# Attention steps in pairs at half as many places of the mixture, one pipeline over three batches, and a set order of the first loads

## The chip, the cores and the metric

The kernel runs on one core of one Trainium2 chip. The metric is device time in microseconds (us) of one execution, as a median of runs. Engines: PE (TensorE), DVE (VectorE), ACT (ScalarE), POOL (GpSimd) and SP (SyncE, which issues most DMAs).

## What is computed

Three layers in a row. The inputs of the mixture (w_a, w_b, w_out) are 64-bit floats, all others 32-bit.

```python
# attention: 4 batches, 8 heads, 576 positions, 64 per head
scores = q @ k.T / 8, masked           # heads 0-3: the last 32 positions
                                       # heads 4-7: every 32nd position before
x = softmax(scores) @ v                # -> 2304 tokens x 512
# gated mixture
x = (x @ w_a) * (x @ w_b) @ w_out      # 512 -> 1536 -> 512
# eight experts, top two of each token
noisy = x @ w_gate + log1p(exp(x @ w_noise)) * noise
for e, w in top2(noisy) with softmax weights w:
    out[token] += w * (relu(x @ w1[e]) @ w2[e])   # 512 -> 1024 -> 512
```

## The kernel before

**Attention.** A batch is four units, each two heads, in the order HPS = (0, 2, 1, 3): hp 0 and 1 have the local mask (96 positions by 128 keys, three at a time), hp 2 and 3 the strided one (72 by 72, four at a time). A unit's steps are T (four, transposes of q and k), Q (four, scores, and behind the second of each half E, the softmax), P (four, transposes of the weights) and PV (two). att_pipe is a generator that yields behind each step and interleaves a unit's with the next one's. Masks are added either by a PE matmul with identb (batch 0) or by a DVE addition (batches 1 to 3, the tensor_add in Q). Where "wide" holds, E is one subtraction, one exponential and one sum over a whole half in place of single rows of ACT with an accumulator.

**Mixture.** Tokens go in chunks: c = 0 to 3 are 512 tokens of one batch each, c = 4 the 4 x 64 left over. A chunk has twelve stages f: stage_a makes pa and pb (12 matmuls each: mm3 multiplies high and low parts in three matmuls), and a*pb in high and low parts gh, gl; stage_b adds to po (12 more, 6 in chunk 4) for the stage before. The 64-bit weights are loaded raw (load_raw, 512 KB or 1 MB) and split on DVE and ACT into high and low parts (split64), 48 steps of it during batch 0 and chunk 0 (conv_to).

**Places.** PE's order is written by hand: stage_a and stage_b call point(), six times a stage: in the middle of pa, behind pa, in the middle of pb, behind pb, and twice in stage_b. Each call advances the attention queue attq by one step, and every third call (every second in chunk 4) the queue bgq, in which finish (X: transposes of the mixture's rows, G: the gate's matmul, then the routing, R: ranks of the tokens in each expert, and eight scatters of the slots to a table in memory), load_expert and fetch (a load of the table, gathers of tokens, S: their transposes) take turns. So the attention of batch c + 1 runs inside chunk c; what is left of it is run at stage 11.

**Other orders.** Except in batch 0, where the scheduler sets it, PE runs what the program says; the other engines' order is set by the scheduler from its own estimate. Expert weights go through two slots st0 and st1 (load_unit, L146; ACT makes the high part, L149, DVE the low part, L150) into the ring slots w0 to w5, which the mixture's stages 0 to 7 hold before. load_expert(0) joins bgq at (c, f) = (4, 5), fetch(0) at (4, 8). Batch 0's q, k, v come through st slots and four more. PSUM tiles of attention, X, G, R and S share the two banks of tag "t"; batch 0's go to the four of tag "o", but for P and PV.

Of the kernel before, what the change touches and what calls it, by code (L numbers as in the profile page):

```python
# [32 lines left out]
def attention_moe_kernel(ctx: ExitStack, tc: tile.TileContext, q, k, v, w_a, w_b, w_out,  # L33
# [165 lines left out]
    class Unit:  # L199
# [36 lines left out]
        def T(self, i):  # L236
# [11 lines left out]
            if self.wide and i // 2:  # L248
# [8 lines left out]
        def Q(self, half, x):  # L257
            n, g, m = self.n, self.g, self.m
            msk = maskAB[:, half:half + 3, :] if self.local else maskS[:, None, :].to_broadcast([72, 4, 72])
            if x == 0:  # L260
                self.s[half] = self.tile("s", [n, 2, g, m])
                st = self.tile("sst", [96, 1 if self.wide else 2, 8])
                self.mx, self.sm[half] = st[:n, 0, 0:2 * g], st[:n, 0 if self.wide else 1, 0:2 * g]
# [3 lines left out]
            if self.pemask:  # L267
                nc.tensor.matmul(ps, identb[:n, :n], msk, start=True, stop=False)
            for ii in range(g):
# [4 lines left out]
                else:  # L274
# [3 lines left out]
                                 start=not self.pemask, stop=not self.pemask or ii == g - 1)  # L278
            mx = self.mx[:, g * x:g * x + g]
            if self.pemask:  # L280
# [10 lines left out]
        def E(self, half):  # L291
            n, g = self.n, self.g
# [3 lines left out]
            if not self.pemask:  # L296
                nc.vector.tensor_reduce(mx, s3, axis=AX.X, op=OP.max)
            if self.wide:
                if not self.pemask:
# [40 lines left out]
    def att_pipe(us, ahead, done=None):  # L340
# [8 lines left out]
        if ahead == 2:  # L349
            us[1].load_v()  # L350
        for n, u in enumerate(us):
# [39 lines left out]
        if done:  # L391
            done(u)
# [111 lines left out]
    pair = [None]  # L504

    def store_x2(c, ps, j):
        if j % 2 == 0:
            pair[0] = rpool.tile([128, 2, DM], F32, name="row", tag=f"row{j // 2}")
        row = pair[0][:, j % 2, :]
# [13 lines left out]
    bgq, attq = [], []  # L523
# [10 lines left out]
    def pump():  # L534
        advance(attq)
        advance(bgq)

    def drain():
        while bgq or attq:
# [22 lines left out]
    def load_m1():  # L562
# [17 lines left out]
    cp = m1.enter_context(tc.tile_pool(name="conv", bufs=1))  # L580
    a1 = ExitStack()
    p1 = a1.enter_context(tc.tile_pool(name="att1", bufs=1, reuse_waits="tile"))
    nraw = [0]

    def next_of(n):
        nraw[0] += 1
        return nraw[0] % n

    conv_room["raw"] = lambda m: cp.tile([128, 1024, 2], I32, name="raw", tag=f"u{next_of(2)}")[:, 0:m, :]
    cts = []  # L590

    def ct_tile(m):

        if not cts:
            ct = cp.tile([128, 2, 1024], I32, name="ct", tag="u2")
            cts.extend((ct[:, 0], ct[:, 1]))
        cts.append(cts.pop(0))
        return cts[-1][:, 0:m]

    conv_room["ct"] = ct_tile  # L600
    conv = load_m1()
    nconv = [0]
# [9 lines left out]
    def p1tile(name, shape):  # L612
        if name in ("ql", "kl", "vl"):
            nslot[0] += 1
            i = nslot[0] % 6
            return stage.tile(shape, F32, name=name, tag=f"st{i}") if i < 2 else \
                p1.tile(shape, F32, name=name, tag=f"qkv{i}")
        return p1.tile(shape, F32, name=name, tag=name, bufs=P1BUFS[name])

# [355 lines left out]
```

## Time and profile before

| | |
|---|---|
| median of the runs | 1170.57 us (1167.08, 1170.57, 1170.78) |
| profiled execution: time, span | 1169.36 us, 1167.6 us |
| PE busy | 1102.8 us, 94% of the span |
| DVE, ACT, POOL busy | 525.3, 418.0, 144.0 us |
| batch 0 up to the first stage of chunk 0 | 0 to 48.7 us |
| chunk 0 | 48.7 to 220.2 |
| chunks 1, 2 (with attention) | 220.2 to 357.5, 357.5 to 494.0 |
| chunk 3 (without) | 494.0 to 599.0 |
| chunk 4 | 599.0 to the first expert matmul, 676.6 |
| expert passes | 676.6 to the end |

Times are from the span's start. A stage's bounds are the first pa matmul of each. The chain of work that ended last is PE for 78% of the span, DMA for 10%, DVE for 7%. A row of the timeline has start, length, engine, line, operation, out<-in, shape and count; in brackets the idle time of the engine just before and what ended it.

### The profile page before, as it was taken

The page shows a single profiled execution, that of the slowest core. Times are in us where ns is not written, and L with a number is a line of the kernel's source. Part 1 is how long each engine was busy: PE and PEld are TensorE (multiplying, and loading weights), DVE is VectorE, ACT ScalarE, POOL GpSimd, SP SyncE. Part 2 cuts the span into 40 slices and gives each one's busy share as a digit, 9 for nine tenths or more (in the row PEclk, how much of TensorE's full clock was granted, in tenths as well). Part 3 has the DMA queues.
Part 4 walks back from the last instruction along what each step waited for, and adds up shares of the span by engine and source line. Part 5 has one row for each costly group of instructions (what it writes and reads, how often), then busy time and mean ns, then how long its engine had stood idle before and what let it go on. Part 6 is the DMA issues. An engine that isn't in the chain of part 4 may idle for free.

```text
span 1167.6 us, 16084 instructions
## 1 busy us (share of the span) xinstructions
PE 1102.8 (94%) x6381; PEld 927.2 (79%) x6381; DVE 525.3 (45%) x1109; ACT 418.0 (36%) x936; POOL 144.0 (12%) x136
## 2 busy tenths in 40 slices
PE   6768999999999999999999699999999998999996
PEld 5546777777777777888888589988999897988995
DVE  5688985355435465211326361245342434242111
ACT  5666664233223242221225251244242424232111
POOL 0000000000200002000020313231030313021112
PEclk9969999999999999999999999999999999999998
DMA  8544522101111111730013643266253626242023
GB/s 183 176 123 153 177 80 65 61 22 32 37 26 58 31 36 49 268 112 1 1 37 110 127 126 57 46 194 183 78 139 92 156 82 166 66 116 40 11 35 48
DMA packets 88549, 105.02 MB, mean 90 GB/s; under 512 B 43664, under 2 KB 48400, under 8 KB 88464
## 3 DMA queue, kind: packets, MB, share of 16 engines
q1 hardware_dynamic: 78352, 82.89, 23.9%
q0 software_dynamic: 10112, 21.02, 9.9%
q8 instruction: 52, 0.85, 0.3%
q14 instruction: 33, 0.27, 0.1%
HBM read 78.53 MB, written 25.35 MB: 89 GB/s over the span
## 4 chain that ended last, share of the span: by engine, by line
PE 78%; DMA 10%; DVE 7%; issue 2%; POOL 2%; ACT 1%; SPq 1%; DVEq 0%; ACTq 0%; POOLq 0%
PE ph L186 6%; PE ph L187 6%; PE ph L188 6%; PE py L186 6%; PE py L187 6%; PE py L188 5%; PE po L186 4%; PE pb L186 4%; PE pa L186 4%; PE pb L188 4%; PE pb L187 4%; PE po L188 4%; PE po L187 4%; PE pa L187 4%; PE pa L188 4%; DMA st<-in_moe_w_dram 3%
## 5 line engine op out<-in xcount | busy, mean ns | idle before, releaser
L825 DVE SCALAR_TENSOR_TENSOR hl<-ph,hh 128x256 fp32r<-128x256 f32 (+1 forms) x128 | 62.1, 488 | 198.2 <-ACT hh L824 197.9
L824 ACT ACTIVATE hh<-ph 128x256 fp32r<-128x256 f32 (+1 forms) x128 | 55.2, 433 | 208.5 <-PE ph L188 208.5
L671 DVE TENSOR_TENSOR a<-a,pb 128x512 f32<-128x512 f32 (+1 forms) x60 | 37.9, 631 | 129.2 <-PE pb L188 129.2
L496 POOL DMA_INDIRECT table<-pay,sli x36 | 35.7, 992 | 452.7 <-DVE sli L483 424.3
L849 POOL DMA_INDIRECT out_dram<-y,tb x40 | 65.1, 1627 | 193.1 <-ACT y L848 127.0
L666 ACT ACTIVATE a<-pa 128x512 f32<-128x512 f32 (+1 forms) x60 | 33.2, 553 | 110.0 <-PE pa L188 107.5
L672 ACT ACTIVATE gh<-a 128x512 fp32r<-128x512 f32 (+1 forms) x60 | 35.3, 588 | 81.2 <-DVE a L671 80.2
L722 POOL DMA_INDIRECT g<-x,tb x40 | 40.6, 1016 | 183.1 <-PE tt L731 165.4
L673 DVE TENSOR_TENSOR gl<-a,gh 128x512 fp32r<-128x512 f32 (+1 forms) x60 | 38.0, 633 | 16.3 <-ACT gh L672 15.8
L277 PEld LDWEIGHTS tt<-kT,qT 64*72 64x72 f32 (+1 forms) x336 | 30.4, 149 | 18.2 <-issue 14.9
L318 PE MATMUL tt<-ident,s 72*72 72x72 f32 (+1 forms) x224 | 30.9, 263 | 11.9 <-DVE s L310 7.8
L318 PEld LDWEIGHTS tt<-ident,s 72*72 72x72 f32 (+1 forms) x224 | 24.4, 141 | 22.4 <-ACT ct L168 4.5
L319 ACT ACTIVATE pT<-tt 128x288 f32<-128x288 f32 (+1 forms) x64 | 25.8, 409 | 42.0 <-PE tt L318 41.6
L277 PE MATMUL tt<-kT,qT 64*72 64x72 f32 (+1 forms) x336 | 39.1, 253 | 0.7 <-DVE s L286 0.7
L186 PE MATMUL py<-w6h,hh 128*128 128x512 f32 x80 | 33.1, 416 | 6.8 <-ACT hh L824 3.6
L331 PEld LDWEIGHTS tt<-pT,vl 72*64 72x64 f32 (+1 forms) x448 | 22.3, 156 | 18.6 <-issue 8.6
L331 PE MATMUL tt<-pT,vl 72*64 72x72 f32 (+1 forms) x448 | 29.8, 270 | 5.6 <-ACT pT L319 5.6
L731 PE MATMUL tt<-ident,g 128*128 128x128 f32 x160 | 26.0, 281 | 9.5 <-DMA g<-x,tb 8.1
L186 PE MATMUL py<-w2h,hh 128*128 128x512 f32 x80 | 33.2, 415 | 0.6 <-DVE y L846 0.6
L186 PE MATMUL pa<-xh,w0h 128*128 128x512 f32 (+1 forms) x80 | 33.6, 420 | 0.0
L731 PEld LDWEIGHTS tt<-ident,g 128*128 128x128 f32 x160 | 20.6, 145 | 15.1 <-DMA g<-x,tb 7.6
L187 PE MATMUL py<-w6l,hh 128*128 128x512 f32 x80 | 32.6, 407 | 0.0
(288 smaller groups left out, 3307.8 us busy)
## 6 DMA issues: line engine op xcount, KB each, us to landing
st<-in_moe_w_dram SPq DMA_DIRECT2D x64, 512.0 KB
out_dram<-zero SPq DMA_DIRECT2D x13, 512.0 KB
raw<-in_moe_w_a_dram SPq DMA_DIRECT2D x4, 1024.0 KB
raw<-in_moe_w_b_dram SPq DMA_DIRECT2D x4, 1024.0 KB
raw<-in_moe_w_out_dram SPq DMA_DIRECT2D x4, 1024.0 KB
x<-row SPq DMA_DIRECT2D x16, 256.0 KB
vl<-in_v_dram SPq DMA_DIRECT2D x16, 160.0 KB
ql<-in_q_dram SPq DMA_DIRECT2D x16, 144.0 KB
```

Of the source, the lines that this page charges most:

```text
L186: nc.tensor.matmul(ps, w[0], x[0], start=start, stop=False)
L187: nc.tensor.matmul(ps, w[0], x[1], start=False, stop=False)
L188: nc.tensor.matmul(ps, w[1], x[0], start=False, stop=stop)
L277: nc.tensor.matmul(ps[:, ii, :], self.qT[r0:r0 + 64, q0:q0 + n], self.kT[r0:r0 + 64, k0:k0 + m], start=not self.pemask, stop=not self.pema ...
L318: nc.tensor.transpose(ps[:, ii, :], self.s[half][:, x, ii, :], ident[:n, :n])
L331: nc.tensor.matmul(ps[64 * hh:64 * hh + 64, jl, :], self.vl[:, hh, g * half + jl, :], self.pT[:, x, ii, :], start=True, stop=True)
L673: nc.vector.tensor_sub(gl, a, gh.bitcast(F32))
L722: nc.gpsimd.indirect_dma_start(out=g, out_offset=None, in_=x2, in_offset=bass.IndirectOffsetOnAxis(ap=TB[e, t][:, 0:1], axis=0))
L731: nc.tensor.transpose(ps[:, kd, :], g[:, 128 * kd:128 * kd + 128], ident)
L824: nc.scalar.activation(hh, ph, AF.Relu)
L825: nc.vector.scalar_tensor_tensor(hl, ph, 0.0, hh.bitcast(F32), op0=OP.max, op1=OP.subtract)
L849: ins = nc.gpsimd.indirect_dma_start(out=out, out_offset=bass.IndirectOffsetOnAxis(ap=TB[e, t][:, 0:1], axis=0), in_=y, in_offset=None, co ...
```

## The change

- point() is called three times a stage: behind pa, behind pb, behind po. Each call advances attention by two steps, or by one and by one step of finish, which has a queue of its own now (finq); bgq advances by one step at each call, in chunk 4 by two.
- Batches 1 to 3 are one att_pipe; PV of a batch waits (may) until the chunk before has given its buffers free.
- Batch 1's masks are added by PE, and ACT copies the scores out ("act"). In batch 0 the second halves of units 1 to 3 are wide.
- Batch 0's q, k, v go to ring slots (slot8), each unit its own, and SP's order in batch 0 is the program's: the loads of all units and the first raw blocks ahead of the rest, raws three ahead into three buffers.
- load_expert(0) joins at (4, 4), fetch(0) at (4, 6). In the expert passes three gathers are in flight, and expert 0's second x set has the room of the rows.

```diff
-        def __init__(self, tile, bank, b, hp, pemask, wide):
-            self.tile, self.bank, self.b, self.hp, self.pemask, self.wide = tile, bank, b, hp, pemask, wide
+        def __init__(self, tile, bank, b, hp, mask, wide):
+            self.tile, self.bank, self.b, self.hp, self.mask, self.wides = tile, bank, b, hp, mask, wide
...
-            if self.pemask:
+            if self.mask == "pe":
                 nc.vector.tensor_reduce(mx, ps, axis=AX.X, op=OP.max)
-                if self.wide:
+                if self.wides[half]:
                     nc.vector.tensor_sub(s[:, x], ps, mx[:, :, None].to_broadcast([n, g, m]))
                 self.src.append(ps)
             else:
-                nc.vector.tensor_add(s[:, x], ps, msk)
+                if pemask:
+                    nc.scalar.activation(s[:, x], ps, AF.Copy)
+                else:
+                    nc.vector.tensor_add(s[:, x], ps, msk)
...
-    def att_pipe(us, ahead, done=None):
+    def att_pipe(us, ahead, done, may=lambda u: True):
...
             us[ahead].load_qk()
-        if ahead == 2:
-            us[1].load_v()
...
-                if done:
-                    done(last)
-                if n + ahead - 1 < len(us):
-                    us[n + ahead - 1].load_v()
+                done(last)
+                if ahead == 1:
+                    u.load_v()
...
+            while not may(u):
+                yield
             u.PV(0)
             yield
...
+        if j == 0:
+            four[0] = rpool.tile([128, 4, DM], F32, name="row", tag="row")
+        row = four[0][:, j, :]
...
-    bgq, attq = [], []
+    bgq, attq, finq = [], [], []
...
+        def ahead(n):
+            while len(raws) < min(n, len(blocks)):
+                raws.append(load_raw(blocks[len(raws)][0], 512 * blocks[len(raws)][2]))
+        conv_room["ahead"] = ahead
+        yield
         for k, (_, f, n, i) in enumerate(blocks):
-            while len(raws) < min(k + 2, len(blocks), 99 if k >= NPAIR else NPAIR):
-                raws.append(load_raw(blocks[len(raws)][0], 512 * blocks[len(raws)][2]))
+            ahead(min(k + (3 if k < NPAIR - 2 else 2), 99 if k >= NPAIR else NPAIR))
...
+    def raw_tile(m):
+
         nraw[0] += 1
-        return nraw[0] % n
-
-    conv_room["raw"] = lambda m: cp.tile([128, 1024, 2], I32, name="raw", tag=f"u{next_of(2)}")[:, 0:m, :]
-    cts = []
-
-    def ct_tile(m):
-
-        if not cts:
-            ct = cp.tile([128, 2, 1024], I32, name="ct", tag="u2")
-            cts.extend((ct[:, 0], ct[:, 1]))
-        cts.append(cts.pop(0))
-        return cts[-1][:, 0:m]
-
-    conv_room["ct"] = ct_tile
+        i = nraw[0] % 3
+        return (cp if i else rpool).tile([128, 1024, 2], I32, name="raw", tag=("row", "u0", "u1")[i])[:, 0:m, :]
...
+            i = nslot[0]
...
+            return slot8(i, shape)
...
+    def slot8(i, shape):
+
+        if i // 2 not in big:
+            big[i // 2] = ring.tile([128, 2, 1024], F32, name=f"qkv{i // 2}", tag=f"w{3 + i // 4}{'hl'[i // 2 % 2]}")
+        n = shape[1] * shape[2] * shape[3]
+        return big[i // 2][:shape[0], i % 2, 0:n].rearrange("p (a b c) -> p a b c", a=shape[1], b=shape[2])
...
-    us = [Unit(p1tile, bank0, 0, hp, True, False) for hp in HPS]
-    us[0].load_qk()
-    us[1].load_qk()
-    us[0].load_v()
-    for i, _ in enumerate(att_pipe(us, 2, lambda u: split_kd(0, u.hp))):
-        conv_to(min(12, 1 + i * 12 // 50))
-    conv_to(12)
+    us = [Unit(p1tile, bank0, 0, hp, "pe", (False, i > 0)) for i, hp in enumerate(HPS)]
+    with tc.manual_schedule(engines={mybir.EngineType.SP}):
+        for i, u in enumerate(us):
+            u.load_qk()
+            u.load_v()
+            conv_room["ahead"](min(i + 1, 3))
+        for i, _ in enumerate(att_pipe(us, 9, lambda u: split_kd(0, u.hp))):
+            conv_to(min(12, i * 12 // 50))
+        conv_to(12)
...
-    def attend(b, wide):
-        us = [Unit(atile, bank1, b, hp, False, wide) for hp in HPS]
-        us[0].load_qk()
-        us[0].load_v()
-        return att_pipe(us, 1)
-
-    attq.append(attend(1, False))
+    us = [Unit(atile, bank1, b, hp, "act" if b == 1 else "dve", (b > 1,) * 2) for b in range(1, B) for hp in HPS]
+    us[0].load_qk()
+    us[0].load_v()
+    attended = set()
+    may = [1]
+    attq.append(att_pipe(us, 1, lambda u: attended.add((u.b, u.hp)), lambda u: u.b <= may[0]))
...
-                if i == 1:
-                    point()
...
-            if 2 * (j + 1) in (J, 2 * J):
-                point()
+        point()
...
+    GB = [2]
...
+            if p is rpool:
+                both = p.tile([128, 2, KD, 128 * n], F32R, name=t, tag="row")
+                XS[e, g] = (both[:, 0], both[:, 1])
+                return XS[e, g]
...
-                    conv_to(n0 + (n1 - n0) * ((npt[0] - 1) % 6 + 1) // 6)
+                    conv_to(n0 + (n1 - n0) * ((npt[0] - 1) % 3 + 1) // 3)
                 advance(attq)
-                if npt[0] % (2 if c == NCH - 1 else 3) == 0:
+                advance(finq if finq else attq)
+                advance(bgq)
+                if c == NCH - 1:
                     advance(bgq)
...
-                while attq:
+                while c + 1 < B and (c + 1, HPS[-1]) not in attended:
...
-            if 0 < c < B - 1 and f == 0:
-                attq.append(attend(c + 1, True))
-            if (c, f) == (NCH - 1, 5):
+            if (c, f) == (NCH - 1, 4):
                 bgq.append(load_expert(0))
-            if (c, f) == (NCH - 1, 8):
+            if (c, f) == (NCH - 1, 6):
                 bgq.append(fetch(0, [0, 1, 2]))
...
+                may[0] = c + 2
...
-                    bgq.append(finish(prev[0], rows))
+                    finq.append(finish(prev[0], rows))
...
+    xpool["g"] = ep
+    GB[0] = 3
...
-    xpool[0, 1] = ep
+    xpool[0, 1] = rpool
```

On SP, at the start of the program, the rows before (ql, kl, vl are slots of q, k, v; raw a block of mixture weights):

```order
L218 DMA ql<-in_q_dram 96x6x64 x2
L218 DMA kl<-in_k_dram 96x6x64 x2
L220 DMA ql<-in_q_dram 72x2x512
L220 DMA kl<-in_k_dram 72x2x512
L226 DMA vl<-in_v_dram 128x2x64
L229 DMA vl<-in_v_dram 128x5x64 x2
L158 DMA raw<-in_moe_w_a_dram 128x4x256
L158 DMA raw<-in_moe_w_b_dram 128x4x256
L218 DMA ql<-in_q_dram 96x6x64 x2
```

and after (ql, kl, vl are now batch 1's first unit, qkv the ring slots of batch 0):

```order
L218 DMA ql<-in_q_dram 96x6x64 x2
L218 DMA kl<-in_k_dram 96x6x64 x2
L226 DMA vl<-in_v_dram 128x2x64
L229 DMA vl<-in_v_dram 128x5x64 x2
L106 DMA wg<-in_moe_w_gate_dram 128x4x8
L218 DMA qkv_162<-in_q_dram 96x6x64 x2
L218 DMA qkv_162<-in_k_dram 96x6x64 x2
L226 DMA qkv_167<-in_v_dram 128x2x64
L229 DMA qkv_167<-in_v_dram 128x5x64 x2
L158 DMA raw<-in_moe_w_a_dram 128x4x256
L220 DMA qkv_167<-in_q_dram 72x2x512
L220 DMA qkv_173<-in_k_dram 72x2x512
```

Batch 0's loads moved behind eight others, and its raws behind all loads of the unit ahead of them.

On PE, in stage 2 of chunk 0, the rows before (pb and po are the mixture, tt the attention of batch 1):

```order
L186 MATMUL pb<-xh,w1h 128x512
L187 MATMUL pb<-xl,w1h 128x512
L188 MATMUL pb<-xh,w1l 128x512
L247 MATMUL tt<-ident,kl 128x72 x4
L186 MATMUL pb<-xh,w1h 128x512
L187 MATMUL pb<-xl,w1h 128x512
L188 MATMUL pb<-xh,w1l 128x512
L186 MATMUL pb<-xh,w1h 128x512
L187 MATMUL pb<-xl,w1h 128x512
L188 MATMUL pb<-xh,w1l 128x512
L247 MATMUL tt<-ident,kl 128x72 x4
L186 MATMUL po<-w2h,gh 128x512
```

and after:

```order
L187 MATMUL pb<-xl,w1h 128x512
L188 MATMUL pb<-xh,w1l 128x512
L186 MATMUL pb<-xh,w1h 128x512
L187 MATMUL pb<-xl,w1h 128x512
L188 MATMUL pb<-xh,w1l 128x512
L247 MATMUL tt<-ident,kl 128x72 x8
L186 MATMUL po<-w2h,gh 128x512
L187 MATMUL po<-w2l,gh 128x512
```

The two transposing steps, which stood in the middle of pb and behind it, stand together behind all twelve matmuls of pb.

On DVE, in chunk 4, around the operands of R (ms) and of the slots (sl), the rows before (w2l, w3l are low parts of expert weights):

```order
L462 TENSOR_TENSOR oh<-iota_76,idf 128x16 x4
L489 TENSOR_SCALAR den<-wt 128x4
L465 TENSOR_TENSOR ms<-oh 128x32
L671 TENSOR_TENSOR a<-a,pb 128x256
L490 RECIPROCAL den<-den 128x4
L491 COPY pay<-den 128x4
L492 TENSOR_TENSOR pay<-wt,den 128x4
L673 TENSOR_TENSOR gl<-a,gh 128x256
L476 TENSOR_TENSOR sl<-tt,base 128x32
L150 TENSOR_TENSOR w3l<-st,w3h 128x512
```

and after:

```order
L150 TENSOR_TENSOR w2l<-st,w2h 128x512
L466 TENSOR_TENSOR oh<-iota_76,idf 128x16 x4
L150 TENSOR_TENSOR w2l<-st,w2h 128x512
L493 TENSOR_SCALAR den<-wt 128x4
L469 TENSOR_TENSOR ms<-oh 128x32
L150 TENSOR_TENSOR w2l<-st,w2h 128x512
L494 RECIPROCAL den<-den 128x4
L150 TENSOR_TENSOR w2l<-st,w2h 128x512
L480 TENSOR_TENSOR sl<-tt,base 128x32
```

The low parts of unit w2 stand among the routing now, two ahead of ms and two ahead of sl; before, w2 lay ahead of all of it.

On POOL, in chunk 4, from the scatters of chunks 0 to 3 (eight each) on, the rows before (g are gathers for the first expert passes):

```order
L496 DMA table<-pay,sli 18432x2 x30
L722 DMA g<-x_57,tb 128x512
L496 DMA table<-pay,sli 18432x2 x2
L722 DMA g<-x_57,tb 128x512 x5
L496 DMA table<-pay,sli 18432x2 x4
```

and after:

```order
L500 DMA table<-pay,sli 18432x2 x32
L747 DMA g<-x_57,tb 128x512 x6
L500 DMA table<-pay,sli 18432x2 x4
L747 DMA g<-x_57,tb 128x512 x3
L877 DMA out_dram<-y,tb 3328x512 x2
```

All 32 scatters stand ahead of the first gather; before, two of chunk 3's stood behind it.

## Rows read from the trace of the kernel before

**Rows 1.** The page, first part: busy us, share of the span, instructions of each engine.
```profile
PE 1102.8 (94%) x6381; PEld 927.2 (79%) x6381; DVE 525.3 (45%) x1109; ACT 418.0 (36%) x936; POOL 144.0 (12%) x136
```

**Rows 2.** Stretches: length, then busy us of each engine, PE's clock, DMA share, GB/s.
```profile
core 0: us, PE busy (x) PEld busy (x) DVE busy (x) ACT busy (x) POOL busy (x), PEclk, DMA share, GB/s
0.00:110.60 110.60, 80.45 (x462) 59.04 (x462) 81.95 (x170) 65.71 (x207) 2.28 (x19) 0.91 0.59 159
599.00:676.60 77.60, 64.20 (x462) 58.11 (x460) 34.47 (x108) 30.00 (x62) 19.04 (x19) 0.96 0.43 106
```

**Rows 3.** Timeline of the start.
```profile
0.76 1.40 SPq L218 DMA_DIRECT2D ql<-in_q_dram  x2
...
4.84 0.29 DVE L81 TENSOR_TENSOR maskAB<-tmp 96x128 bf16<-96x128 f32 x1
...
5.16 1.20 PE L247 MATMUL sc<-ident,ql 96*128 96x96 f32 x6 [5.16 <-DMA ql<-in_q_dram]
```

**Rows 4.** Timeline of PE in stage (0, 2): the first P of batch 1.
```profile
110.73 0.71 PE L318 MATMUL tt<-ident,s 96*128 96x96 f32 x3 [4.09 <-DVE s L310]
```

**Rows 5.** DVE's groups, 0 to 110.6 us: count, busy us, mean ns, idle before.
```profile
L281 DVE TENSOR_REDUCE sst<-sc 72x4 f32<-72x288 f32 x8 | 3.4, 445 | 0.0
...
L286 DVE TENSOR_TENSOR s<-tt,maskAB 96x384 f32<-96x384 f32 x4 | 2.2, 548 | 0.0
```

**Rows 6.** What the first step of split64 (L167, DVE) waited for: us, times.
```profile
  DMA raw<-in_moe_w_a_dram: 6.0, 4
```

**Rows 7.** Timeline of PE at two places of chunk 0: a T, a pair Q.
```profile
116.93 0.40 PE L188 MATMUL pb<-xh,w1l 128*128 128x512 f32 x1
117.16 0.41 PE L247 MATMUL tt<-ident,kl 72*128 72x72 f32 x4
117.38 0.48 PE L186 MATMUL po<-w2h,gh 128*128 128x512 f32 x1
117.70 0.40 PE L187 MATMUL po<-w2l,gh 128*128 128x512 f32 x1
...
120.87 0.40 PE L188 MATMUL po<-w2h,gl 128*128 128x512 f32 x1
121.20 0.73 PE L277 MATMUL tt<-kT,qT 64*72 64x72 f32 x8
121.86 0.50 PE L186 MATMUL pa<-xh,w0h 128*128 128x512 f32 x1
122.20 0.39 PE L187 MATMUL pa<-xl,w0h 128*128 128x512 f32 x1
```

**Rows 8.** Timeline of PE in batch 0: a mask matmul and its scores.
```profile
44.91 0.55 PE L268 MATMUL sc<-maskAB,identb 96*96 96x384 bf16 x1
45.39 1.17 PE L277 MATMUL sc<-kT,qT 64*96 64x128 f32 x4
```

**Rows 9.** Timeline of chunk 4: expert 0's weights, R, S.
```profile
616.71 1.15 ACT L149 ACTIVATE w0h<-st 128x512 fp32r<-128x512 f32 x2 [2.19 <-PE pa L187]
...
633.03 1.29 DVE L150 TENSOR_TENSOR w2l<-st,w2h 128x512 fp32r<-128x512 f32 x2 [0.53 <-ACT w2h L149]
...
640.24 0.18 PE L470 MATMUL tt<-ms,tri 128*128 128x8 bf16 x1
...
669.95 1.12 PE L731 MATMUL tt<-ident,g 128*128 128x128 f32 x4 [7.41 <-DMA g<-x,tb]
```

**Rows 10.** Timeline of SP and POOL: the table's load, the fifth scatter.
```profile
655.58 0.34 SPq L716 DMA_DIRECT2D tb<-table  x1
...
659.46 1.28 POOL L496 DMA_INDIRECT table<-pay,sli  x1 [9.67 <-issue]
```

**Rows 11.** The chain of waits: start, us, what; DMA steps last to their landing.
```profile
604.05 0.97 POOL table L496
...
612.94 4.74 DMA table<-pay,sli
...
662.31 7.59 DMA g<-x,tb
...
671.34 3.27 DMA g<-x,tb
```

More of the change, by code (lines that the diff above doesn't have):

```diff
@@ L247, in T @@
                 nc.tensor.transpose(ps[:, jj, :], src[:, g * half + jj, :, :], ident[:n, :n])
-            if self.wide and i // 2:
+            if self.mask == "dve" and i // 2:
                 nc.vector.tensor_copy(dv[:, g * half:g * half + g, :], ps)
@@ L261, in Q @@
                 self.s[half] = self.tile("s", [n, 2, g, m])
-                st = self.tile("sst", [96, 1 if self.wide else 2, 8])
-                self.mx, self.sm[half] = st[:n, 0, 0:2 * g], st[:n, 0 if self.wide else 1, 0:2 * g]
+                wide = self.wides[half]
+                st = self.tile("sst", [96, 2, 8])
+                self.mx, self.sm[half] = st[:n, 0, 0:2 * g], st[:n, 1, 0:2 * g]
                 self.src = []
@@ L266, in Q @@
             ps = self.bank("Q", [n, g, m])
-            if self.pemask:
+            pemask = self.mask != "dve"
+            if pemask:
                 nc.tensor.matmul(ps, identb[:n, :n], msk, start=True, stop=False)
@@ L291, in E @@
         def E(self, half):
+            wide = self.wides[half]
             n, g = self.n, self.g
@@ L295, in E @@
             over = lambda a: a[:, :, None].to_broadcast(list(s3.shape))
-            if not self.pemask:
+            if self.mask != "pe":
                 nc.vector.tensor_reduce(mx, s3, axis=AX.X, op=OP.max)
-            if self.wide:
-                if not self.pemask:
+            if wide:
+                if self.mask != "pe":
                     nc.vector.tensor_sub(s3, s3, over(mx))
@@ L390, in att_pipe @@
         u.PV(1)
-        if done:
-            done(u)
+        done(u)
         yield
@@ L502, in route @@
             yield
-    pair = [None]
+    four = [None]
     def store_x2(c, ps, j):
-        if j % 2 == 0:
-            pair[0] = rpool.tile([128, 2, DM], F32, name="row", tag=f"row{j // 2}")
-        row = pair[0][:, j % 2, :]
+        if j == 0:
+            four[0] = rpool.tile([128, 4, DM], F32, name="row", tag="row")
+        row = four[0][:, j, :]
         if j % 2:
@@ L534, in pump @@
     def pump():
-        advance(attq)
+        advance(finq)
         advance(bgq)
     def drain():
-        while bgq or attq:
+        while bgq or finq:
             pump()
@@ L580, in attention_moe_kernel, with halves, get @@
     cp = m1.enter_context(tc.tile_pool(name="conv", bufs=1))
+    att = ExitStack()
+    apool = att.enter_context(tc.tile_pool(name="att", bufs=1, side="right"))
     a1 = ExitStack()
-    p1 = a1.enter_context(tc.tile_pool(name="att1", bufs=1, reuse_waits="tile"))
+    p1 = a1.enter_context(tc.tile_pool(name="att1", bufs=1))
     nraw = [0]
-    def next_of(n):
+    def raw_tile(m):
         nraw[0] += 1
-        return nraw[0] % n
-    conv_room["raw"] = lambda m: cp.tile([128, 1024, 2], I32, name="raw", tag=f"u{next_of(2)}")[:, 0:m, :]
-    cts = []
-    def ct_tile(m):
-        if not cts:
-            ct = cp.tile([128, 2, 1024], I32, name="ct", tag="u2")
-            cts.extend((ct[:, 0], ct[:, 1]))
-        cts.append(cts.pop(0))
-        return cts[-1][:, 0:m]
-    conv_room["ct"] = ct_tile
+        i = nraw[0] % 3
+        return (cp if i else rpool).tile([128, 1024, 2], I32, name="raw", tag=("row", "u0", "u1")[i])[:, 0:m, :]
+    def halves(pool, shape, name, tag):
+        t = []
+        def get(m):
+            if not t:
+                both = pool.tile([shape[0], 2] + shape[1:], I32, name=name, tag=tag)
+                t.extend((both[:, 0], both[:, 1]))
+            t.append(t.pop(0))
+            return t[-1][:, 0:m]
+        return get
+    conv_room["raw"] = raw_tile
+    conv_room["ct"] = halves(cp, [128, 1024], "ct", "u2")
     conv = load_m1()
+    next(conv)
     nconv = [0]
@@ L613, in p1tile @@
         if name in ("ql", "kl", "vl"):
+            i = nslot[0]
             nslot[0] += 1
-            i = nslot[0] % 6
-            return stage.tile(shape, F32, name=name, tag=f"st{i}") if i < 2 else \
-                p1.tile(shape, F32, name=name, tag=f"qkv{i}")
+            return slot8(i, shape)
         return p1.tile(shape, F32, name=name, tag=name, bufs=P1BUFS[name])
+    big = {}
+    def slot8(i, shape):
[3 more added lines that the diff above has]
+        return big[i // 2][:shape[0], i % 2, 0:n].rearrange("p (a b c) -> p a b c", a=shape[1], b=shape[2])
     def bank0(name, shape):
@@ L720, in gather @@
     def gather(e, t):
-        g = xpool["g"].tile([128, DM], F32, name="g", tag="g", bufs=2)
+        g = xpool["g"].tile([128, DM], F32, name="g", tag="g", bufs=GB[0])
         nc.gpsimd.indirect_dma_start(out=g, out_offset=None, in_=x2,
@@ L765, in attention_moe_kernel @@
                 last_units(cp, 10, ("u0", "u1", "u2"))
-                conv_room["raw"] = lambda m: rpool.tile([128, 512, 2], I32, name="raw", tag=f"row{next_of(2)}")
+                conv_room["raw"] = halves(rpool, [128, 512, 2], "raw", "row")
                 conv_room["ct"] = lambda m: rpool.tile([128, 512], I32, name="ct", tag="x2T")
             if f == NF - 1:
-                while attq:
+                while c + 1 < B and (c + 1, HPS[-1]) not in attended:
                     advance(attq)
@@ L894, in overflow_tile @@
         nc.vector.tensor_copy(x, ps)
-        h = ep.tile([128, NF2, 128], F32, name="hf", tag="x11h")
+        h = ep.tile([128, NF2, 128], F32, name="hf", tag="hf")
         for f in range(NF2):
```

10 lines of the change are left out of this document (4 added, 6 removed).

## The prediction

> **What bounds the kernel now.** I read the page's first part, then the idle times of TensorE (PE), then, for each long one, the timeline around it. PE is busy 94% of the span [rows 1], so time changes only where PE waits, or where an instruction on PE grows or goes. Two stretches hold most of what the change touches. The first 110.6 us, where batch 0 is computed and the first mixture stages run: PE is busy 80.45 us of them, VectorE (DVE) 81.95 [rows 2]. And chunk 4, from 599.0 to the first expert matmul at 676.6: PE is busy 64.20 of 77.60, so it idles 13.4 us [rows 2]. In between PE has hardly a gap; there the change acts through the cost of its places alone.
>
> The profiled execution took 1169.36 us, span 1167.6; the median of the runs, 1170.57, is 1.2 us above it. The sum below stands on 1169.36. About 0.3% (3.5 us) is what a measurement of this kernel can tell from no change.
>
> **Start: the first loads.** Before, the first q is issued at 0.76, the first transpose runs at 5.16 [rows 3]. After, SP issues eight other DMAs first (unit 0 of batch 1, the gate's weights), and batch 0's first q waits on DVE: its slot lies in the ring, over the setup's scratch, whose last mask write is 4.84 + 0.29 = 5.13 [rows 3]. From there the same 4.4 us (5.16 - 0.76) lead to the first transpose: 9.5 to 10, so **+4.8 us** before DVE's first work on scores. Queued behind that wait on SP is every load of batch 0 and every raw weight block.
>
> **Early DVE.** The first P of batch 1 on PE waits 4.09 us for the last multiply of a softmax on DVE [rows 4]. The same multiply is just as far down DVE's order after (some 160 rows). So this end is DVE's work plus DVE's idle time. Work: six wide subtractions and three wide sums come in, each priced by the nearest rows, a maximum over scores and an addition on them, near 0.5 us for one half of a score tile and twice that for both [rows 5]: 6 x 0.5 + 3 x 0.9 = 5.7. Four mask additions of 0.548 (2.2) and some small scalings (0.2) go, and the last subtractions and sums lie behind that multiply (some 1.3): 82 + 2 = 84. Idle: 110.6 - 82 = 28.6 before, of which 17.8 wait for raw weight blocks (6.0 for w_a's as shown, and 5.9 for each of the two other weights') [rows 6] and 6.6 is the start. After, the start is 6.6 + 4.8 = 11.4. The raw blocks are issued three ahead into three buffers, but the first of them issues 13th on SP and not third, and each later one stands behind the three to seven loads of a unit, so I leave 10 to 18 of the 17.8, and take 13. With 1 us for the rest: 84 + 11.4 + 13 + 1 = 109.4, against 110.73. Bounds: 105 to 114 by the idle time, and PE itself would not come there before 106.6 (110.73 - 4.09). What is late next if DVE is early is PE's own work. Term: **-1.5** (-7 to +8, the lower end where the waits of PE ahead of it go as well).
>
> **Pairs.** A place between two groups of mixture matmuls costs more than the attention step in it: after a transposing place the next mixture matmul but one starts 0.32 after the first, where 0.23 is the pace (116.93 to 117.16 against 117.38 to 117.70); a score place pays 0.33 going in and 0.34 coming out (120.87 to 121.20, 121.86 to 122.20) [rows 7]. Merging two transposing places saves some 0.09, two score or PV places some 0.19. From the order, 167 places with attention become 101: 66 fewer, about 30 of the first kind and 36 of the second at most, 2.7 + 6.8 = 9.5 if each saved in full; places that merge a score with a transposition, or attention with the router's step, save about half. Sum **-4.8** (-11 to -2). The row shows the extra 0.09. The Trainium skill, TensorE: Matmul & The Clock Gate, section "What happens when you issue a matmul", says that PE pulls weight loads ahead of the matmuls in flight, so that a switch of operands would cost nothing and this term would be 0; by it the sum would be 4.8 higher. The spacing in [rows 7] does not agree with it, and I go by the rows.
>
> **Mask on PE in batch 1.** Sixteen mask matmuls come in, 45.39 - 44.91 = 0.48 us from one's start to the next work [rows 8]; others overlap more, 0.4 on average: 16 x 0.4 = 6.4. Four of them lie ahead of the DVE-bound wait at 110 and cost nothing while it stands: **+4.8** (0 to +7). They take DVE additions of 0.548 off and put copies of the same tile on ScalarE, 36% busy [rows 1]. Pairs and masks together: **0** (-11 to +5).
>
> **Two steps on two banks.** "t" has two PSUM banks. A pair fills both at once, so the next place needs both evacuated, which single steps did not. The three places of a stage lie twelve mixture matmuls, 12 x 0.23 = 2.8 us, apart, and an evacuation is one operation of some 0.5 us [rows 5], so most fit; where both go through one engine that has other work, PE waits: **+1** (0 to +5; the far end is a rival).
>
> **Chunk 4.** Four things move together. (1) R, the rank matmuls of chunk 3's tokens, moves from (4,7) to the end of (4,4). Before, it ran at 640.24 without a wait [rows 9]. After, its operand (ms, L469) stands on DVE behind the third weight unit's first two conversions. Those hang on the first conversion, 616.71, which needs the ring slot that stage (4,3) frees; it is the same slot after. The third unit's second pair came at 633.03 [rows 9], 16.3 later, the first pair 2.2 before that. So ms is ready about 17.3 us after (4,3) begins (1.6 + 15.5 + 0.2), and PE, with (4,3) and (4,4) of some 5 us each, is there at 10: PE waits **7.5**. Queued behind R on PE is all of (4,5). (2) sl (L480) stands behind the other pair, so the slots (sli) come at 20. (3) All eight scatters stand ahead of the table load, where before four did and the fifth waited behind it for 9.67 us [rows 10]. Eight took 612.94 - 604.05 + 4.74 = 13.6 us from the first's start to the last's landing [rows 11]. The load took 3.9 (655.58 to 659.46) [rows 10], a gather 3.27 to 7.59 [rows 11]. That puts the first gathered tile at 20.5 + 13.6 + 3.9 + 3.3 to 7.6 = 41.3 to 45.6. (4) The first spread, S, moves from behind the last stage to (4,7), behind its pa. PE has two stages and 1.4 us, some 10 us, between R and S: it arrives at 17.5 + 10 = 27.5 and waits 13.8 to 18. Before, R to S were 29.7 us, with four stages and more between, and still 7.41 of waiting [rows 9]. Sum of the new waits 21.3 to 25.5 against the 13.4 that chunk 4 has now, if those all go: +8 to +12, a little less if PE's granted clock, which is 0.96 over this stretch [rows 2], does not fall again. I take **+9** (+1 to +13). The rows on transfers here are longer than the Trainium skill's: DMA: Bandwidth & Descriptors, section "Anatomy of one DMA — SWDGE (gpsimd) path", gives about 2.0 us and the bytes at 436 GB/s, so an estimate from it is 2.6 for the 256 KB gather and 2.0 for a scatter's landing. By it the term would be about +4 and the sum 1172; the 7.59 of [rows 11] speaks against it.
>
> **Expert passes.** PE's order there is nearly the same; a third gather buffer and an own room for one x set can ease or shift single waits of 3 us: 0 (-4 to +4).
>
> **Sum:** 1169.36 - 1.5 + 0 + 1 + 9 + 0 = 1177.9; I give **1177**.
>
> **Rivals.**
> A, the forecast: chunk 4's chain grows into two waits. For it: the order and the lengths of [rows 9 to 11].
> B, the raw waits go: with three buffers the 17.8 us of [rows 6] vanish, the end of [rows 4] moves to PE's own pace, and the early term is -8 in place of -1.5: 1177 - 6.5 = 1170.5. Against it: the late start of all loads.
> C, the other side: the gathers are there before PE is. If PE's work between R and S, or what R waits for, covers the chain, both waits stay small, and the stalls of chunk 4 as it stands go with the early gather: -9.4 (four of 13.4 kept) in place of +9: 1177 - 18.4 = 1158.6. It decides if R to the gather's landing takes under about 10 us; 29.7 is what [rows 9] show, and the shortest sum of parts, with no wait for DVE, is 25.
> D, the two banks: pairs wait for evacuations in most stages, 36 stages x 0.3: +10, so 1187.
> E, a short chain: R does not wait (ms gets ahead by the loads landing sooner) and the gather takes 3.3: the waits are 14 to 15.5 against 13.4, the term is +2, 1170.
>
> **How the numbers follow.** A 0.44, B 0.15, C 0.18, D 0.12, E 0.11. The likeliest is A, so 1177; its own range is 1171 to 1186. Of A 0.08 falls within 0.3% of the median (up to 1174.1); of B 0.09 and of E 0.08 do, the rest of these is faster. Faster: 0.18 + 0.06 + 0.03 = 0.27; same 0.25; slower 0.36 + 0.12 = 0.48. The range, 1160 to 1188, leaves out most of C and the end of D.
>
> **What would show it.** Right: first transpose at 9 to 10 us; the first P of batch 1 between 105 and 114; spacing of mixture matmuls unbroken over 12, stages of chunks 1 to 3 about as long as before in batch 1 and shorter by 0.2 us a stage later; in chunk 4 a wait of PE on DVE ahead of R and one of over 12 us on the gather ahead of S in (4,7), and none behind (4,11). Wrong: S without a wait (C); waits of P or T on ScalarE's copies in most stages (D); the first P of batch 1 before 104 (B).

## The result, and the profile after

The changed kernel takes 1159.54 us (median of five runs, 1157.78 to 1162.07) against 1170.78 of the kernel before, measured beside it: a ratio of 0.9899, with a 95% interval of 0.9866 to 0.9932, 11 to 12 us faster. The forecast was 1177, with a range of 1160 to 1188.

The profiled execution of it took 1162.07, the slowest of its five, with a span of 1160.2; that of before 1169.36, close to its median. So the two profiles show 7.4 of the difference. Cut at the same places of the program, they read:

| stretch | before | after | difference | forecast |
|---|---|---|---|---|
| start to stage (0, 3) | 121.9 | 121.9 | 0.0 | -1.5 |
| (0, 3) to the end of chunk 3 | 477.1 | 473.2 | -3.9 | +1 (pairs, masks, two banks) |
| chunk 4 | 77.6 | 80.4 | +2.8 | +9 |
| expert passes | 491.0 | 484.7 | -6.3 | 0 |

The same stretches of after by engine; columns as in [rows 2], the seventh number is PE's granted clock.

```profile
0.00:110.78 110.78, 81.81 (x472) 60.79 (x473) 84.18 (x170) 65.34 (x181) 2.29 (x19) 0.98 0.59 158
...
121.90:595.10 473.20, 472.35 (x2748) 378.91 (x2748) 225.32 (x490) 163.18 (x361) 23.83 (x25) 1.00 0.21 64
595.10:675.50 80.40, 63.70 (x442) 59.61 (x442) 34.17 (x100) 29.19 (x60) 10.79 (x11) 0.87 0.33 102
675.50:1160.20 484.70, 469.31 (x2680) 424.48 (x2678) 167.94 (x327) 150.20 (x300) 104.89 (x81) 0.99 0.41 98
```

PE works through the second stretch almost without a gap, after as before; what it gained there is work. Chunk 4 has 16.7 us without work (80.40 - 63.70), 13.4 before [rows 2].

The waits of PE that the forecast named, in the timeline of after:

```profile
10.08 1.19 PE L247 MATMUL sc<-ident,qkv 96*128 96x96 f32 x6 [10.08 <-DMA qkv<-in_q_dram]
...
110.78 0.55 PE L324 MATMUL tt<-ident,s 96*128 96x96 f32 x2 [6.25 <-DVE sst L314]
...
629.48 0.19 PE L474 MATMUL tt<-ms,tri 128*128 128x8 bf16 x1 [6.61 <-DVE ms L469]
...
652.69 0.48 PE L756 MATMUL tt<-ident,g 128*128 128x128 f32 x1 [10.10 <-DMA g<-x,tb]
```

All four came about, though not all in the size that the prediction set as its sign: it asked for over 12 us ahead of S, and for 9 to 10 at the start. The first transpose runs at 10.08 (5.16 before, [rows 3]); the first P of batch 1 runs at 110.78 (110.73, [rows 4]); R waits 6.61 for its operand (none before, [rows 9]); S waits 10.10 for a gather (7.41 behind the last stage, [rows 9]). The kernel is faster in spite of them. The gain lies in the expert passes, where the forecast put nothing, and in the second stretch, where it put +1.

### The profile page after: what moved, and what is told of

It is laid out like the page before. It is cut to its first block, busy times and chain, and to the rows that moved or that the text cites. A ratio compares the mean times of both kernels' runs of the same rounds, so it can differ in the third digit from the quotient of the medians.

```text
span 1160.2 us, 16083 instructions
## 1 busy us (share of the span) xinstructions
PE 1098.3 (95%) x6397; PEld 932.6 (80%) x6397; DVE 522.7 (45%) x1099; ACT 413.7 (36%) x911; POOL 141.8 (12%) x136
## 5 line engine op out<-in xcount | busy, mean ns | idle before, releaser
L877 POOL DMA_INDIRECT out_dram<-y,tb x40 | 64.3, 1608 | 180.1 <-ACT y L876 136.8
L756 PE MATMUL tt<-ident,g 128*128 128x128 f32 x160 | 25.8, 277 | 11.9 <-DMA g<-x,tb 10.1
L186 PE MATMUL pb<-xh,w1h 128*128 128x512 f32 (+1 forms) x80 | 33.0, 413 | 0.0
L186 PE MATMUL pb<-xh,w4h 128*128 128x512 f32 (+1 forms) x80 | 32.1, 401 | 0.0
L187 PE MATMUL pa<-xl,w0h 128*128 128x512 f32 (+1 forms) x80 | 31.1, 389 | 0.8 <-DVE xl L404 0.8
```

Of the source, the lines that this page charges most:

```text
L186: nc.tensor.matmul(ps, w[0], x[0], start=start, stop=False)
L187: nc.tensor.matmul(ps, w[0], x[1], start=False, stop=False)
L756: nc.tensor.transpose(ps[:, kd, :], g[:, 128 * kd:128 * kd + 128], ident)
L877: ins = nc.gpsimd.indirect_dma_start(out=out, out_offset=bass.IndirectOffsetOnAxis(ap=TB[e, t][:, 0:1], axis=0), in_=y, in_offset=None, co ...
```

## The experiments

Each is compared with runs of the kernel before that were made beside it; differences to the changed kernel are those of the ratios, times 1170. Both ratios have an interval, so such a difference is good to 4 or 5 us either way, and one smaller than that can't be told from none. A profile shows one execution, and a stretch of it can differ by some us between executions.

**One part undone: the third gather buffer (e1), and it alone on the kernel before (e8).** e1:

```diff
     xpool["g"] = ep
-    GB[0] = 3
```

> The changed kernel with two gather buffers in the expert passes as before, all else as changed. In the profiles the expert passes (first expert matmul to the end) fell from 491.0 to 484.7 us, 6.3 of the 7.4 by which the spans differ. Theory G, the third gather buffer did it: the passes are back at 489 to 492 and the time is 1164 to 1167, with a wait of PE on an evacuation of y. Rival K, the passes shifted by chance or by what chunk 4 hands them: passes 483 to 486, time 1158 to 1161.

Measured: 1168.42, ratio 0.9981 (0.9962 to 1.0), 9.6 over the changed kernel (1.4 over the range of G); passes 491.4, with the wait on y:

```profile
986.94 0.80 PE L186 MATMUL py<-w6h,hh 128*128 128x512 f32 x1 [2.94 <-ACT y L875]
```

Theory G holds for the passes. e8 leaves all of before as it is, and gives the expert passes a third tile for gathers from the pool "e":

```diff
+        GB[1] += 1
+        if GB[0] == 3 and GB[1] % 3 == 0:
+            g = ep_box[0].tile([128, DM], F32, name="g", tag="g3")
+        else:
+            g = xpool["g"].tile([128, DM], F32, name="g", tag="g", bufs=2)
...
-            if len(gs) == 2:
+            if len(gs) == GB[0]:
```

> The kernel before with a third gather buffer in the expert passes and nothing else. Theory G, the third buffer alone is worth what it gave in the changed kernel: passes 483 to 486 in place of 491.0, time 1162 to 1165. Rival K, it needs what else the change did there (the order in which chunk 4 hands over, the room of the x set): passes 489 to 492, time 1168 to 1171.

Measured: 1163.88, ratio 0.9928 (0.9904 to 0.9953), 8.4 off; passes 482.1. Again G: the buffer alone, in either kernel, is worth 8 to 10 us, the greater part of the whole result. The passes of all the profiles say the same: 491.0 and 491.4 with two buffers (before and e1), 480.5 to 484.7 with three (the changed kernel, e8 and all other experiments). Where it goes can be read in the timeline of before, where the pass of expert 4 ends and that of expert 5 begins (py are the second matmuls, y their evacuation):

```profile
978.12 0.60 PE L731 MATMUL tt<-ident,g 128*128 128x128 f32 x4
...
983.54 1.01 POOL L722 DMA_INDIRECT g<-x,tb  x1 [0.30 <-issue]
...
987.43 0.69 ACT L848 ACTIVATE y<-py,tb 128x512 f32<-128x512 f32 x1 [4.75 <-issue]
...
988.17 0.79 PE L186 MATMUL py<-w6h,hh 128*128 128x512 f32 x1 [3.19 <-ACT y L848]
```

A gather (POOL, 983.54) stands among the five scatters of y, ACT copies the last y out of PSUM at 987.43, and PE waits 3.19 for that bank. The fifth py of an expert takes one of the two banks of tag "t", which the S tiles share. An S (978.12) stands between the old expert's fifth py and the new one's, and the new one then meets the old one's bank. Late in the wait the granted clock falls to its lower level: it is 0.50 from 987.6 to 994.2. The rows are that stretch and the 15 us around it in before, then the same 15 us in e1, where the wait is shorter:

```profile
987.60:994.20 6.60, 6.03 (x17) 5.05 (x18) 1.58 (x3) 1.77 (x4) 2.58 (x2) 0.50 0.97 223
985.00:1000.00 15.00, 11.83 (x52) 10.39 (x53) 3.01 (x6) 3.03 (x7) 4.49 (x3) 0.77 0.62 143
```

```profile
985.00:1000.00 15.00, 13.06 (x66) 11.59 (x67) 3.26 (x6) 3.41 (x7) 3.97 (x4) 0.89 0.57 140
```

After, a gather is issued at 968, ahead of the scatters. The last y is copied about as late, at 987.91, so the gather's place is not what delays that copy. But no S stands between 967.29 and 988.63: PE comes to that bank later in its order, with an S and not with a second matmul, and waits 0.41:

```profile
967.29 0.60 PE L756 MATMUL tt<-ident,g 128*128 128x128 f32 x4
...
968.16 0.95 POOL L747 DMA_INDIRECT g<-x,tb  x1 [5.02 <-PE tt L756]
...
987.91 0.67 ACT L876 ACTIVATE y<-py,tb 128x512 f32<-128x512 f32 x1
988.63 0.66 PE L756 MATMUL tt<-ident,g 128*128 128x128 f32 x4 [0.41 <-ACT y L876]
```

That one pass took 66.1 us before (971.1 to 1037.2), 58.3 after, 64.3 in e1 and 58.7 in e8. (The profile of e8 is one of its slower executions, 1165.95, and 5.5 longer than before's up to the passes; the 8.4 rests on the medians.) The number of buffers also sets behind how many gathers the first S stands, so that e1 and e8 move the order of PE together with the buffer; the order alone, with two buffers, was not tried.

**Pairs undone (e2).** The same sequence of steps, one at each of six places:

```diff
                 mm3(ps, tuple(t[:, kd, cols] for t in w), xT[c, kd], i == 0, i == KD - 1)
+                if i == 1:
+                    point()
...
-        point()
+            if 2 * (j + 1) in (J, 2 * J):
+                point()
...
-                advance(attq)
+                if npt[0] % 2:
+                    advance(attq)
+                    return
```

> The changed kernel with six places a stage again, one step at each, in the same sequence of steps. Theory P, the pairs save time because fewer places break the mixture: chunk 0 from its fourth stage on and chunks 1 and 2, 367.8 us together after and 372.1 before, are longer by 4 to 10 us, time 1164 to 1169. Rival N, a place costs as little as weight loads that run beside matmuls, and the gain in these chunks comes from the one pipeline or the wide forms: 366 to 370 us there, time 1158 to 1161.

Measured: 1163.14, ratio 0.9947 (0.9927 to 0.9967), 5.6 over the changed kernel, just under the range of P. From (0, 3) to the end of chunk 3 its PE is busy all the time, 478.9 against 473.2:

```profile
116.40:595.30 478.90, 478.90 (x2750) 376.96 (x2749) 229.20 (x491) 165.10 (x361) 23.78 (x25) 1.00 0.21 62
```

Theory P: the pairs are worth 5.7 us of PE's time there. By a count of the trace, other work breaks the mixture there at 102 places in the changed kernel, 179 in e2 and 160 before, so e2 undoes more than the change did: an estimate for the change is 58/77 of 5.7, or 4.3. Three other kernels that have the changed kernel's code there (e1, e5, e6) take 473.3 each. But ahead of (0, 3) e2 is the shorter, 116.4 against 121.9 (119.4 to 121.8 in those three): the first P of batch 1 stands at 104.15, and DVE's splits wait 6.2 us for raw blocks, not 10.4. So in chunk 0's first stages the pairs seem to cost some 3 to 5 us. The profile of e2 is its fastest execution (1160.31), and why its median is 5.6 over is not shown by the stretches alone.

The mask matmuls can be priced in the changed kernel itself, from the start of one to the start of the next work:

```profile
124.78 0.29 PE L270 MATMUL tt<-maskS,identb 72*72 72x288 bf16 x1
125.00 0.47 PE L279 MATMUL tt<-kT,qT 64*72 64x72 f32 x4
...
148.03 0.36 PE L270 MATMUL tt<-maskAB,identb 96*96 96x384 bf16 x1
148.32 0.46 PE L279 MATMUL tt<-kT,qT 64*96 64x128 f32 x2
```

All sixteen take 0.22 to 0.29 us, 4.0 together, not 0.4 each.

**Masks of batch 1 back on DVE (e3), and so with the start mended (e11).**

```diff
-    us = [Unit(atile, bank1, b, hp, "act" if b == 1 else "dve", (b > 1,) * 2) for b in range(1, B) for hp in HPS]
+    us = [Unit(atile, bank1, b, hp, "dve", (b > 1,) * 2) for b in range(1, B) for hp in HPS]
```

> The changed kernel with batch 1's masks added by DVE again (no mask matmul, no copy on ScalarE there). Theory M, the sixteen mask matmuls cost PE 0.4 us each, of which four lie ahead of the wait for DVE at 110.8: stages of chunk 0 after that 4 to 5 us shorter, the wait at 110.8 longer by four additions of 0.55, 2 us: time 1156 to 1158. Rival W, DVE is what sets the pace of chunk 0, and the additions cost more than the matmuls: time 1161 to 1164.

> As e4 (batch 0's loads first), with batch 1's masks added by DVE as in e3. Theory W, DVE's work sets the pace of chunk 0, and the additions lengthen it whatever the start: 1156 to 1160, 4 to 8 over e4. Rival X, the 7.0 us that PE waited at 149 us in e3 were one meeting of a softmax with a raw block that came late, and without it the mask matmuls only cost PE time: 1148 to 1152.

Measured: e3 1167.19, ratio 0.9974 (0.9956 to 0.9991), 8.8 over the changed kernel; e11 1163.76, ratio 0.9934 (0.9908 to 0.9959), 9.7 over e4. Theory M falls, and X's times do not come out either: the second wait is there in both kernels. Both times are 3 to 4 us above the ranges of W, too, so its direction holds and not its size. The timeline of e3, DVE's rows ahead of it, and PE's two waits in e11:

```profile
144.07 0.69 DVE L167 TENSOR_SCALAR ct<-raw 128x1024 int32<-128x1024 int32 x1 [2.65 <-DMA raw<-in_moe_w_out_dram]
...
146.49 0.19 DVE L315 RECIPROCAL sst<-sst 72x8 f32<-72x8 f32 x1
...
148.29 0.75 DVE L316 TENSOR_TENSOR s<-s,sst 72x576 f32<-72x576 f32 x1
...
149.19 0.43 PE L324 MATMUL tt<-ident,s 72*72 72x72 f32 x2 [7.03 <-ACT gh L693]
```

```profile
107.30 0.39 PE L326 MATMUL tt<-ident,s 96*128 96x96 f32 x1 [8.70 <-DVE sst L316]
...
143.67 0.31 PE L326 MATMUL tt<-ident,s 72*72 72x72 f32 x1 [7.71 <-ACT gh L697]
```

The last steps of a softmax stand on DVE behind a split that waits for a raw block, and P waits for them; the releaser named, gh, is the last of several. Sixteen additions of about half a us on DVE, spread over some 170 us, cost 9 to 10 us, and the profiles have it in these two waits: the first is 8.08 in e3 and 6.25 in the changed kernel, 8.70 in e11 and 2.81 in e4; the second is in neither of the two without the additions. The second is one meeting of a softmax with a late raw block, in both kernels, so what the additions would cost without it stays open. The kernel before had the same additions and no such wait (its longest between 121.9 and 599.0 was 0.84); which other part of the change (the raws three ahead, the wide halves, the pairs) leaves DVE this little room was not tried apart.

**The first loads (e4).** The ring is told to wait tile by tile for the setup's scratch, and batch 1's first loads, the gate's weights and the noise are issued behind batch 0's:

```diff
-    ring = ctx.enter_context(tc.tile_pool(name="ring", bufs=1))
+    ring = ctx.enter_context(tc.tile_pool(name="ring", bufs=1, reuse_waits="tile"))
...
             conv_room["ahead"](min(i + 1, 3))
+        us1[0].load_qk()
+        us1[0].load_v()
+        late_loads()
```

> The changed kernel with batch 0's loads first: the ring waits for the setup tile by tile, so the first q waits for nothing, and batch 1's first loads, the gate's weights and the noise are issued behind batch 0's. Theory S, the first loads cost 4.8 us at the start that reach the wait of PE on DVE at 110.8: first transposes at 5 to 5.5, that wait ends at 105 to 107, time 1154 to 1156. Rival R, raw blocks bind DVE all the same (10.4 us of its idle time up to there): it ends at 109 to 111, time 1158 to 1161.

Measured: 1151.78, ratio 0.9851 (0.9821 to 0.9882), 5.6 under the changed kernel. The profile has 8.1 less: 9.7 gained ahead of (0, 3), 1.6 given back behind it (S waits 12.65 there, not 10.10):

```profile
5.09 0.39 PE L249 MATMUL sc<-ident,qkv 96*128 96x96 f32 x1 [5.09 <-DMA qkv<-in_q_dram]
...
102.30 0.27 PE L326 MATMUL tt<-ident,s 96*128 96x96 f32 x1 [2.81 <-DVE sst L316]
```

Theory S, and more than it asked for: the transposes come 5.0 earlier, the end of the wait on DVE 8.5. DVE had 3.3 us less to do ahead of it (80.84 busy up to 102.3, 84.18 up to 110.78): the order of its work moved too.

**No wide softmax in batch 0 (e7).**

```diff
-    us = [Unit(p1tile, bank0, 0, hp, "pe", (False, i > 0)) for i, hp in enumerate(HPS)]
+    us = [Unit(p1tile, bank0, 0, hp, "pe", (False, False)) for i, hp in enumerate(HPS)]
```

> The changed kernel with no wide softmax in batch 0 (rows of ScalarE with an accumulator in place of one subtraction, one exponential and one sum). Theory D, DVE sets the end of the early stretch: 5.7 us of DVE's work go, the wait of PE at 110.8 ends at 105 to 108, time 1154 to 1157. Rival A, ScalarE's rows (0.35 and 0.19 us each, eight to a half) are what the raw blocks and the evacuations then wait for: it ends at 110 or later, time 1159 to 1164.

Measured: 1160.43, ratio 0.9904 (0.9879 to 0.993): no difference to the changed kernel's 0.9899. The wait ends at 110.28, not at 105 to 108; DVE is busy 82.73 of it, only 1.5 less than with the wide halves, since the steps of one more split (3.0 us) came ahead in their place. Theory D falls. The numbers are those of rival A, but that ScalarE's rows are what holds the end up is not shown: the wait ends with DVE's work, as in the changed kernel.

**Chunk 4: the fetch later (e5), and R later too (e6).**

```diff
-            if (c, f) == (NCH - 1, 4):
+            if (c, f) == (NCH - 1, 6):
                 bgq.append(load_expert(0))
-            if (c, f) == (NCH - 1, 6):
+            if (c, f) == (NCH - 1, 9):
                 bgq.append(fetch(0, [0, 1, 2]))
```

> The changed kernel with the fetch for expert 0 joining at stage (4, 9) in place of (4, 6) (and load_expert(0) at (4, 6)); the first S then stands in (4, 10). Theory C, S waits because two stages of PE's work lie between R and S and the chain takes 23.2 us: with five stages the wait of 10.1 falls to 0 to 3, the wait of R (6.6) stays, chunk 4 takes 70 to 74 us in place of 80.4, time 1149 to 1153. Rival H, the wait is handed on to the later S or to the first expert matmul: chunk 4 takes 77 us or more, time 1156 to 1160.

Measured: 1149.44, ratio 0.9804 (0.9778 to 0.983), 11.1 under the changed kernel; chunk 4 takes 69.8. The edit moves load_expert(0) too, but the conversions that R's operand stands behind are where they were (w0h at 614.59 against 614.58, w2h at 626.93 against 626.46), so it is the later fetch that bears on S. R waits 7.07, S 1.11:

```profile
629.95 0.19 PE L474 MATMUL tt<-ms,tri 128*128 128x8 bf16 x1 [7.07 <-DVE ms L469]
...
661.70 0.30 PE L756 MATMUL tt<-ident,g 128*128 128x128 f32 x1 [1.11 <-issue]
```

e6 adds idle steps ahead of R, so that it stands at the end of (4, 6), and lets the fetch join at (4, 10):

```diff
         yield
+        for _ in range(6 if c == B - 1 else 0):
+            yield
         rk = pt([128, J + 1, 8])
```

> The changed kernel with R of chunk 3 two stages later, at the end of (4, 6), and the fetch joining at (4, 10), so that S stands in (4, 10) and (4, 11). Theory C, R waits because its operand stands behind the low parts of unit w2 on DVE: there the operand is ready and R waits 0 to 1; R to S leaves some 17 us of PE's work for a chain of 23, S waits 3 to 7: chunk 4 takes 67 to 72, time 1146 to 1151. Rival H, waits are only handed on, to the first expert matmul or to R (whose operand comes as late as before after PE): 77 or more, time 1156 to 1160.

Measured: 1152.99, ratio 0.9836 (0.9811 to 0.9862), 7.4 under; chunk 4 takes 72.6. R waits no more, at 628.95, and S waits 10.07 all the same:

```profile
656.71 0.48 PE L758 MATMUL tt<-ident,g 128*128 128x128 f32 x1 [10.07 <-DMA g<-x,tb]
```

The chain from R took 27.8 us here, with only four stages of PE's work beside it, so the wait moved from R to S. The table's load is issued 20.6 us behind R (649.51), 15.1 in the changed kernel. The size was missed (3 to 7 expected, and 1152.99 lies above the range of C), the rule that PE's work between R and S has to cover the chain was not.

**Both together (e9, e10).** e9 has the edits of e4 and e5; e10 those of e4, R at the end of (4, 6), load_expert(0) at (4, 6) and the fetch at (4, 11).

> The changed kernel with both: batch 0's loads first, as in e4, and the fetch at (4, 9), as in e5. If the two costs are apart, the gains add: 7.8 and 10.1 off 1159.5, 1140 to 1144. If they are not (the start's gain is given back at a later wait), 1146 or more.

> As e9, but with R two stages later, at the end of (4, 6), and the fetch at (4, 11), so that S stands behind the last pb as in the kernel before. Theory C: R no longer waits for its operand, and the gathered tiles are there when PE comes to S (23 to 27 us behind R): chunk 4 takes 63 to 66 in place of 80.4, time 1135 to 1140. Rival H: the first expert matmuls now wait for the spread tiles or for weights, chunk 4 takes 70 or more, time 1142 or more.

Measured: e9 1140.89, ratio 0.9741 (0.9716 to 0.9765); e10 1142.14, ratio 0.9752 (0.9728 to 0.9777). The two gains add. In e10 neither R nor S waits long, but the last stages do, among loads and conversions, and chunk 4 takes 73.1 (70.2 in e9). The 63 to 66 of its theory C did not come; the numbers are those of rival H, though the waits stand on the last stages and an S, not on the first expert matmuls that H named:

```profile
638.61 0.50 PE L188 MATMUL po<-w,gh 128*128 128x512 f32 x1 [2.94 <-ACT gh L699]
...
653.69 0.33 PE L762 MATMUL tt<-ident,g 128*128 128x128 f32 x1 [2.26 <-DMA g<-x,tb]
```

e9 is 30 us under the kernel before and 18 under the changed one; e9 and e10 are not told apart.

## Why the prediction was wrong, point by point

The sum stood on the profile of before and came to 1177.9; the profile of after took 1162.07, 15.8 less. By the table the expert passes make 6.3 of it, chunk 4 6.2 and the second stretch 4.9; the early stretch goes the other way with 1.5.

**Expert passes, "0 (-4 to +4)": the step that failed.** The third gather buffer was named and called an ease of single waits of 3 us. It took away one such wait and the low clock behind it, and the runs give it 8 to 10 us (e1, e8), the difference between a forecast of no gain and the one measured. What the trace was able to show beforehand was there: PE's wait of 3.19 on an evacuation of y at 988.17 and the 0.77 of its clock behind it. I had read that wait and not asked what in the change bears on it, because PE's order in the passes is nearly the same; "nearly" was the point: where S stands among the matmuls decides which bank PE meets. Whether the room of the third buffer or that order alone does it stays open.

**Pairs, "-4.8 (-11 to -2)": right for the stretch that it priced.** e2 gives 5.6, its profile 5.7 behind (0, 3), of which an estimate of 4.3 is the change's, so the spacing in [rows 7] was a fair price. What the pairs seem to cost ahead of (0, 3), 3 to 5 us in e2's profile, was not in the term. The Trainium skill's rule (TensorE: Matmul & The Clock Gate, "What happens when you issue a matmul"), that weight loads are pulled ahead of the matmuls in flight, does not make a place free in these runs, as those 5.7 us show.

**Masks, "+4.8 (0 to +7)": wrong size, and the wrong engine.** PE paid 0.22 to 0.29 us a mask in the changed kernel, some 3 for the twelve that the term counted. The row I took, 0.48 from one start to the next, is from batch 0, where no mixture matmul stands beside it. And DVE, without them, has room that it lacks with them (e3, e11): my term counted the cost to PE and nothing for DVE, and so put the cover the wrong way round. Pairs and masks by these prices make -1.3 and not the 0 of the forecast; PE's idle time in the stretch, 1.56 before and 0.85 after, makes another -0.7 of the -3.9 measured. The cause of the rest, some 2 us of PE's work, stays open.

**Two banks, "+1 (0 to +5)":** no such wait shows; PE is busy 472.35 of the 473.20 us.

**Early stretch, "-1.5 (-7 to +8)": right in its sum, 0.0, in part by luck.** DVE's work was forecast at 84 and is 84.18; the raw blocks' waits at 13 and are 10.4, all other idle time at 12.4 and is 16.2; the first transpose at 9.5 to 10 and is at 10.08; the end at 109.4 and is at 110.78. But e7 shows that taking work off DVE need not move the end, since its order fills up; and the order of the first loads, priced at 4.8, held that end up by 8.5 (e4).

**Chunk 4, "+9 (+1 to +13)": the mechanism was right, the size was off.** R waits 6.61 (7.5 forecast). S waits 10.10 (13.8 to 18). The two rows that differ: the gather took 3.36 us, the short end of 3.3 to 7.6, and PE came to S later, 13.1 us of work behind R and not 10, because its clock in that stretch was lower. Over the work itself it is 0.76, and 13.1 x 0.76 is 10:

```profile
629.50:642.60 13.10, 13.09 (x86) 12.30 (x86) 4.00 (x17) 2.78 (x7) 7.77 (x8) 0.76 0.31 83
629.50:652.70 23.20, 13.10 (x87) 12.32 (x87) 6.58 (x21) 5.14 (x11) 9.84 (x10) 0.72 0.40 107
```

16.7 without work against 13.4 make 3.3, and the stretch is 2.8 longer. The Trainium skill's fit for such transfers (DMA: Bandwidth & Descriptors, "Anatomy of one DMA — SWDGE (gpsimd) path") gave an estimate of 2.6 for the gather; the 3.36 here is nearer to it than the 7.59 of [rows 11] that I set against it. e5 shows what the early fetch costs: 11 us.

**The rivals.** The time fell where C had put it, for another reason: in C the gathers were to be there before PE, and they were not. No rival had the expert passes as its place. B did not come about (10.4 of the 17.8 us of raw waits stayed), nor D, nor E (R waited).

## What to carry to other kernels

Go through the edits one by one and ask of each wait in the profile whether the edit can reach it; a line like "one more buffer" at the end of a diff can carry most of the result. Before a step is moved earlier, add up the chain that its operand hangs on and PE's work in between: where the work is the shorter, the move buys a wait. And where one engine sets a stretch's pace, price an addition to it at what it delays, not at its own length.

## What was not expected of the hardware

A wait of 3.19 us on PE went with a mean granted clock of 0.77 (of 2.4 GHz; the lower level is 1.2) over the 15 us around it in the kernel before, and one of 2.94 us with 0.89 in e1. The pass around it was 7.8 us longer than after, of which 3.2 are the wait. An estimate of what the lower clock takes is half of the 6.6 us at 0.50 (987.6 to 994.2), 3.3; the pass of before also holds one more S, and the rest, under a us, is not accounted for. In chunk 4 the same shows between the waits of R and S, 6.6 and 10.1 us: 0.72 over 629.5 to 652.7.
